# MLP layers: the split, conversion and load of weights are emitted behind a layer-in group instead of in front of it

## The chip, the cores and the metric

The kernel runs on one core of one Trainium2 chip. The metric is the device time of one execution in microseconds (us). TensorE (PE) does the matrix products, VectorE (DVE), ScalarE (ACT) and GpSimd (POOL) the elementwise work, and SyncE (SP) issues the DMAs.

## The reference

```python
def _moe_ref(x, w_in, w_out):                 # x: 1152 tokens x 512
    h = x @ w_in                              # 512 x 2048
    g = np.maximum(0.01 * h, h)
    return (g @ w_out).astype(np.float32)     # 2048 x 512

def _moe2_ref(x, w_in, w_out):
    h = x @ w_in
    g = h * (1.0 / (1.0 + np.exp(-h)))
    return (g @ w_out).astype(np.float32)

def reference(**kwargs):
    attn_out = _attn_ref(**attn_kwargs)       # 2 batches x 8 heads, queries pooled by 2
    x = np.ascontiguousarray(attn_out.transpose(0, 2, 1, 3)).reshape(B * S, H * D)
    x = _moe_ref(x=x, **moe_kwargs)
    return _moe2_ref(x=x, **moe2_kwargs)
```

The four weight matrices arrive as 64-bit floats.

## The kernel before

Attention fills roughly the first 274 us of the program; the two MLP layers fill the rest. The change touches the MLP layers alone.

**Precision and weights.** Every product is made of three matmuls, high by high, high by low and low by high, so each operand exists as a high and a low tile. The weights are cut into 64 *pieces* of 128 x 512. `Weights.load` (L106) fetches one piece as raw 64-bit words into one of 3 buffers. `Weights.convert` turns it into 32-bit floats in one ACT instruction (L127) and four DVE instructions (L131, L135, L139, L145). `Weights.split` makes the high tile on ACT (L163) and the low tile on POOL (L167). The three calls stand together as split, convert, load: the split takes the piece that the call before it converted, the convert takes the next one.

**Units and phases.** A *unit* is (layer, block of the 2048 hidden columns, token group): 2 layers x 4 blocks x 2 groups = 16 units. Group 0 has 512 tokens, group 1 has 640 in two chunks of 320. The loop over `ph` runs 17 *phases*. In phase `ph` the four `layer_in` groups of unit `ph` (here in0 to in3: 12 or 24 matmuls, L923) are interleaved with the output groups of unit `ph - 1` (out0 to out3, or out4: L957 in layer 0, L985 in layer 1) in the order of `phase_order`. The usual one is in0, in1, out0, in2, out1, in3, out2, out3 (, out4). Phase 8 is the first of layer 1; it has in0, in1, out0 to out3, in2, in3. Layer 1 has group 0 in even phases and group 1 in odd ones.

**What follows a group.** In layer 0 ACT alone takes a finished `layer_in` group out of PSUM (L938, L939) and POOL makes the low part `gl` (L944). In layer 1 it takes a chain: a sigmoid on ACT (L941), `a = h * t` on DVE (L942), the copy `gh` on ACT (L943), `gl` on POOL (L944). An output group is added to its accumulator on DVE (L971 in layer 0, L996 in layer 1); for the first block of a layer ACT copies it (L969, L994). At the end of layer 0 each output group is also written as the next layer's input, `xh` on ACT (L973) and `xl` on POOL (L974). The text writes a(ph,i) for the L942 instruction of group in`i` in phase `ph`.

**What sets the order.** In the MLP layers each engine executes its instructions in the order in which this code emits them; there is no planner there. The PSUM pool `ps_p` has 4 buffers, used in rotation by in and out groups alike, so a group on PE starts only when the group four places earlier has been taken out of PSUM. Phases 0 to 2 have a count of weight steps of their own; from phase 3 on there is one split, convert and load for each `layer_in` group until the pieces run out, in phase 14.

Of the kernel before, what the change touches and what calls it, by code (L numbers as in the profile page):

```python
# [18 lines left out]
@with_exitstack  # L19
def pooled_attention_two_mlps(  # L20
    ctx: ExitStack,
    tc: tile.TileContext,
    q: bass.AP,
    k: bass.AP,
    v: bass.AP,
    w1_in: bass.AP,
    w1_out: bass.AP,
    w2_in: bass.AP,
    w2_out: bass.AP,
    out: bass.AP,  # L30
):
    nc = tc.nc
    B, H, S, D = q.shape
    NT, DM = out.shape
    DFF = w1_in.shape[1]
    outer = ctx.enter_context(tc.tile_pool(name="outer", bufs=1))
    KDM = DM // 128
    xh = outer.tile([128, KDM, NT], F32R, name="xh")
    xl = outer.tile([128, KDM, NT], F32R, name="xl")
    weights = Weights(ctx, tc, ((w1_in, w1_out), (w2_in, w2_out)), DM, DFF)  # L40
    with tc.manual_schedule():
        attention(tc, q, k, v, xh, xl, weights)
        mlps(tc, xh, xl, weights, out)
# [20 lines left out]
    weights=(-3.0, -0.3),  # L64
# [827 lines left out]
def mlps(ctx, tc, xh, xl, weights, out):  # L892
# [107 lines left out]
    def phase_order(ph, ins, outs):  # L1000

        if not ins or not outs:
            return ins + outs
        if ph == 2 * NBLK - 1:
            return ins[0:1] + outs[0:2] + ins[1:2] + outs[2:] + ins[2:]
        if ph == 2 * NBLK:
            return ins[0:2] + outs + ins[2:]
        if ph == 4 * NBLK - 1:
            return ins[0:3] + outs[0:1] + ins[3:] + outs[1:]
        order = ins[0:1]  # L1010
        for i in range(max(len(ins) - 1, len(outs))):
            order = order + ins[i + 1:i + 2] + outs[i:i + 1]
        return order
# [4 lines left out]
    for ph in range(len(units) + 1):  # L1018
        ins, outs = [], []
        if ph < len(units):  # L1020
            u = units[ph]
            ins = [(layer_in, u, f) for f in range(FB)]
        if ph > 0:
            w = units[ph - 1]
            if w[0] == 0:
                outs = [(layer_out_t, w, m) for m in range(KDM)]
            else:
                outs = [(layer_out, w, i) for i in range(groups[w[2]][1] * groups[w[2]][2] // 128)]
        order = phase_order(ph, ins, outs)
        for x, u, i in order:  # L1030
            if x is layer_in and ph > 2:
                weights.split()
                weights.convert()
                weights.load()
            x(u, i)
            if x is layer_in and ph == 2:
                weights.split()
                weights.convert()
                weights.load()
            if x is layer_in and ph < 2:  # L1040
                for _ in range((PARAMS["moe0"], PARAMS["moe1"])[ph][i]):
                    weights.convert()
                    weights.load()
                weights.split()
# [29 lines left out]
```

## Time and profile before

| what | value |
|---|---|
| median of 3 runs | 687.91 us (686.66 to 688.94) |
| time of the profiled execution | 688.05 us |
| its span in the trace | 686.3 us |
| mean granted TensorE clock | 0.985 of full speed |
| busy: PE, DVE, POOL, ACT | 657.7, 466.6, 398.9, 321.7 us |

The span is the time between the first and the last recorded instruction; the run's own time is 1.75 us longer. Busy time of an engine is an average over stages that have different limits, so it is read stage by stage below. All times in the rows are us from the start of the span.

### The profile page before, as it was taken

The page shows a single profiled execution, that of the slowest core. Times are in us where ns is not written, and L with a number is a line of the kernel's source. Part 1 is how long each engine was busy: PE and PEld are TensorE (multiplying, and loading weights), DVE is VectorE, ACT ScalarE, POOL GpSimd, SP SyncE. Part 2 cuts the span into 40 slices and gives each one's busy share as a digit, 9 for nine tenths or more (in the row PEclk, how much of TensorE's full clock was granted, in tenths as well). Part 3 has the DMA queues.
Part 4 walks back from the last instruction along what each step waited for, and adds up shares of the span by engine and source line. Part 5 has one row for each costly group of instructions (what it writes and reads, how often), then busy time and mean ns, then how long its engine had stood idle before and what let it go on. Part 6 is the DMA issues. An engine that isn't in the chain of part 4 may idle for free.

```text
span 686.3 us, 10321 instructions
## 1 busy us (share of the span) xinstructions
PE 657.7 (96%) x3741; PEld 533.7 (78%) x3741; DVE 466.6 (68%) x689; ACT 321.7 (47%) x694; POOL 398.9 (58%) x303
## 2 busy tenths in 40 slices
PE   6899999999979988999999999999989999999997
PEld 4566776767756754898988989999878898898986
DVE  6775758577789979497667567367666578877222
ACT  5446667575737555464533334244434543334120
POOL 7476888878868984565454354364634444455220
PEclk9899999999999999999999999999989999999999
DMA  5535151534634123032322223113122322220012
GB/s 147 154 79 140 36 139 37 156 80 125 182 84 120 49 63 105 5 124 93 123 92 78 77 94 91 62 60 95 61 77 78 92 93 69 88 89 1 0 47 92
DMA packets 41898, 59.71 MB, mean 87 GB/s; under 512 B 15324, under 2 KB 24568, under 8 KB 41848
## 3 DMA queue, kind: packets, MB, share of 16 engines
q1 hardware_dynamic: 41848, 59.07, 29.6%
q8 instruction: 29, 0.48, 0.3%
q14 instruction: 21, 0.17, 0.1%
HBM read 49.81 MB, written 2.42 MB: 76 GB/s over the span
## 4 chain that ended last, share of the span: by engine, by line
PE 76%; DVE 13%; issue 4%; ACT 4%; DMA 2%; SPq 1%; ACTq 0%; DVEq 0%
PE ph L923 25%; PE po L957 13%; PE pf L985 12%; PE pss L634 9%; PE pv L666 9%; PE pmx L580 4%; DVE mx L584 3%; PE prep L431 2%; DVE wt L135 2%; DVE wt L139 2%; DVE wt L131 2%; DVE a L942 1%; ACT wt L127 1%; DVE ql L488 1%; DVE wt L145 1%
## 5 line engine op out<-in xcount | busy, mean ns | idle before, releaser
L944 POOL TENSOR_TENSOR gl<-a,gh 128x512 fp32r<-128x512 f32 (+1 forms) x64 | 95.1, 1488 | 163.4 <-ACT gh L943 107.5
L655 POOL TENSOR_TENSOR acc<-acc,e 128x576 f32<-128x576 f32 x105 | 154.7, 1494 | 33.2 <-ACT e L638 27.4
L638 ACT ACTIVATE e<-pss 128x288 f32<-128x288 f32 x288 | 101.8, 411 | 84.9 <-PE pss L634 80.7
L584 DVE TENSOR_REDUCE mx<-pmx 128x1 f32<-128x384 f32 x216 | 110.5, 550 | 33.7 <-PE pmx L580 29.1
L923 PE MATMUL ph<-xh,w0h 128*128 128x320 f32 (+1 forms) x384 | 109.7, 340 | 4.2 <-DVE a L942 3.6
L923 PE MATMUL ph<-xl,w0h 128*128 128x320 f32 (+1 forms) x384 | 109.3, 339 | 0.0
L923 PE MATMUL ph<-xh,w0l 128*128 128x320 f32 (+1 forms) x384 | 109.0, 338 | 0.0
L131 DVE TENSOR_SCALAR wt<-wt 128x512 f32<-128x512 f32 x64 | 51.0, 797 | 81.4 <-ACT wt L127 72.6
L634 PE MATMUL pss<-qh,k 128*128 128x288 f32 x288 | 87.8, 321 | 2.2 <-DVE mx L584 2.0
L666 PE MATMUL pv<-e,vnat 128*64 128x288 f32 x576 | 87.7, 425 | 1.2 <-ACT e L638 1.2
L634 PE MATMUL pss<-ql,ka 128*128 128x288 f32 x288 | 82.2, 301 | 4.3 <-DMA ql<-mn 4.3
L923 PEld LDWEIGHTS ph<-xh,w0h 128*128 128x128 f32 x384 | 68.4, 191 | 12.0 <-DVE a L942 4.7
L923 PEld LDWEIGHTS ph<-xh,w0l 128*128 128x128 f32 x384 | 67.7, 190 | 5.0
L923 PEld LDWEIGHTS ph<-xl,w0h 128*128 128x128 f32 x384 | 67.9, 191 | 4.7
L634 PEld LDWEIGHTS pss<-qh,k 128*128 128x128 f32 x288 | 55.4, 192 | 20.2 <-issue 8.3
L580 PE MATMUL pmx<-k,qh 128*128 128x384 f32 x192 | 66.0, 383 | 4.9 <-DVE mx L584 3.0
L943 ACT ACTIVATE gh<-a 128x512 fp32r<-128x512 f32 (+1 forms) x32 | 22.0, 687 | 95.1 <-DVE a L942 95.1
L145 DVE SCALAR_TENSOR_TENSOR wt<-wraw,wt 128x512 uint32<-128x512 uint32 x64 | 62.6, 978 | 2.0
L135 DVE TENSOR_SCALAR wt<-wt 128x512 uint32<-128x512 uint32 x64 | 62.0, 970 | 2.1
L139 DVE SCALAR_TENSOR_TENSOR wt<-wraw,wt 128x512 uint32<-128x512 uint32 x64 | 58.7, 917 | 2.0
L666 PEld LDWEIGHTS pv<-e,vnat 128*64 128x64 f32 x576 | 35.6, 138 | 31.3 <-issue 14.3
L634 PEld LDWEIGHTS pss<-ql,ka 128*128 128x128 f32 x288 | 55.6, 193 | 5.0 <-DMA ql<-mn 3.0
(76 smaller groups left out, 1126.5 us busy)
## 6 DMA issues: line engine op xcount, KB each, us to landing
wraw<-in_moe_w_in_dram SPq DMA_DIRECT2D x32, 512.0 KB, 3.8
wraw<-in_moe_w_out_dram SPq DMA_DIRECT2D x32, 512.0 KB, 3.3
vnat<-in_v_dram SPq DMA_DIRECT2D x8, 576.0 KB, 4.8
qnat<-in_q_dram SPq DMA_DIRECT2D x16, 256.0 KB, 6.2
knat<-in_k_dram SPq DMA_DIRECT2D x7, 576.0 KB, 4.2
ka<-k SPq DMA_DIRECT2D x16, 160.0 KB, 2.6
out_dram<-acc SPq DMA_DIRECT2D x9, 256.0 KB, 2.0
ka<-k SPq DMA_DIRECT2D x16, 128.0 KB, 2.6
```

The lines of the kernel that those rows point to most:

```text
L135: nc.vector.tensor_scalar(out=t, in0=t, scalar1=4, scalar2=1, op0=ALU.logical_shift_left, op1=ALU.logical_shift_right)
L139: nc.vector.scalar_tensor_tensor(out=t, in0=box["high"], scalar=0x80000000, in1=t, op0=ALU.bitwise_and, op1=ALU.bitwise_or)
L580: nc.tensor.matmul(out=ps[:, 0:KC], lhsT=QH[p, j][:, t * 128:(t + 1) * 128], rhs=K2[p, j][:, ks], start=True, stop=True)
L584: nc.vector.tensor_reduce(out=mx[p][:, n:n + 1], in_=ps[:, 0:KC], op=ALU.max, axis=AX.X)
L634: nc.tensor.matmul(out=ps[:, 0:C], lhsT=lhsT[:, ks], rhs=rhs[:, cs], start=not last, stop=last)
L638: nc.scalar.activation(out=e_t[p, j, t][:, cs], in_=ps[:, 0:C], func=ACTF.Exp, scale=scale)
L655: e.tensor_tensor(out=acc[p, j], in0=e_t[p, j, 0] if t == 1 else acc[p, j], in1=e_t[p, j, t], op=ALU.add)
L666: nc.tensor.matmul(out=vps[p, c][own[j], 0:C], lhsT=vnat[p][:, j, t, :], rhs=e_t[p, j, t][:, c * C:(c + 1) * C], start=(t == 0), stop=(t = ...
L923: nc.tensor.matmul(out=ps[:, c, 0:n], lhsT=wt[:, kk, fs], rhs=m[:, kk, chunk(g, c)], start=(kk == 0 and wt is wh and m is xh), stop=(kk == ...
L944: nc.gpsimd.tensor_tensor(out=gl[:, 0:nch * n], in0=a, in1=gh[:, 0:nch * n], op=ALU.subtract)
L957: nc.tensor.matmul(out=ps[:, c, 0:n], lhsT=wt[:, f, ms], rhs=x[:, c * n:(c + 1) * n], start=(f == 0 and wt is oh and x is gh), stop=(f == ...
L985: nc.tensor.matmul(out=ps[:, 0, :], lhsT=x[:, ts], rhs=wt[:, f, :], start=(f == 0 and x is gh and wt is oh), stop=(f == FB - 1 and x is gl),)
```

## The change

The three weight calls stood ahead of a `layer_in` group for `ph > 2` and behind it for `ph == 2`. Now they stand behind it for every `ph >= 2`. No instruction is added or removed.

```diff
         for x, u, i in order:
-            if x is layer_in and ph > 2:
-                weights.split()
-                weights.convert()
-                weights.load()
             x(u, i)
-            if x is layer_in and ph == 2:
+            if x is layer_in and ph >= 2:
                 weights.split()
                 weights.convert()
                 weights.load()
```

The first place is DVE in phase 12, layer 1, from behind a(12,0) to the accumulation of out1. `a_...` is the product with the sigmoid (L942), `wt_...` the piece in conversion (its four instructions), `pf_...` a finished output group that L996 adds to the accumulator. Before:

```order
L131 TENSOR_SCALAR wt_6097<-wt_6097 128x512
L135 TENSOR_SCALAR wt_6097<-wt_6097 128x512
L139 SCALAR_TENSOR_TENSOR wt_6097<-wraw_5942,wt_6097 128x512
L145 SCALAR_TENSOR_TENSOR wt_6097<-wraw_5942,wt_6097 128x512
L942 TENSOR_TENSOR a_6119<-ph_6105,t_6118 128x512
L996 TENSOR_TENSOR acc1_3469<-pf_6126,acc1_3469 128x512
L131 TENSOR_SCALAR wt_6142<-wt_6142 128x512
L135 TENSOR_SCALAR wt_6142<-wt_6142 128x512
L139 SCALAR_TENSOR_TENSOR wt_6142<-wraw_6001,wt_6142 128x512
L145 SCALAR_TENSOR_TENSOR wt_6142<-wraw_6001,wt_6142 128x512
L942 TENSOR_TENSOR a_6164<-ph_6150,t_6163 128x512
L996 TENSOR_TENSOR acc1_3469<-pf_6171,acc1_3469 128x512
```

The accumulation of an output group stands right behind the product a of the group before it, and in front of the next conversion. The same place with the change:

```order
L942 TENSOR_TENSOR a_6109<-ph_6095,t_6108 128x512
L131 TENSOR_SCALAR wt_6118<-wt_6118 128x512
L135 TENSOR_SCALAR wt_6118<-wt_6118 128x512
L139 SCALAR_TENSOR_TENSOR wt_6118<-wraw_5975,wt_6118 128x512
L145 SCALAR_TENSOR_TENSOR wt_6118<-wraw_5975,wt_6118 128x512
L996 TENSOR_TENSOR acc1_3469<-pf_6126,acc1_3469 128x512
L942 TENSOR_TENSOR a_6154<-ph_6140,t_6153 128x512
L131 TENSOR_SCALAR wt_6163<-wt_6163 128x512
L135 TENSOR_SCALAR wt_6163<-wt_6163 128x512
L139 SCALAR_TENSOR_TENSOR wt_6163<-wraw_6034,wt_6163 128x512
L145 SCALAR_TENSOR_TENSOR wt_6163<-wraw_6034,wt_6163 128x512
L996 TENSOR_TENSOR acc1_3469<-pf_6171,acc1_3469 128x512
```

Now the accumulation stands between the end of a conversion and the next product a.

The second place is DVE in phase 8, where layer 1 begins: from a(8,1) to a(8,2), with the four accumulations of layer 0's last output groups (`po_...`, L971). Before:

```order
L942 TENSOR_TENSOR a_5225<-ph_5211,t_5224 128x512
L971 TENSOR_TENSOR acc1_3469<-po_5232,acc1_3469 128x640
L971 TENSOR_TENSOR acc1_3469<-po_5260,acc1_3469 128x640
L971 TENSOR_TENSOR acc1_3469<-po_5288,acc1_3469 128x640
L971 TENSOR_TENSOR acc1_3469<-po_5316,acc1_3469 128x640
L131 TENSOR_SCALAR wt_5346<-wt_5346 128x512
L135 TENSOR_SCALAR wt_5346<-wt_5346 128x512
L139 SCALAR_TENSOR_TENSOR wt_5346<-wraw_5136,wt_5346 128x512
L145 SCALAR_TENSOR_TENSOR wt_5346<-wraw_5136,wt_5346 128x512
L942 TENSOR_TENSOR a_5368<-ph_5354,t_5367 128x512
```

A conversion stands between the last accumulation and a(8,2). With the change:

```order
L942 TENSOR_TENSOR a_5215<-ph_5201,t_5214 128x512
L131 TENSOR_SCALAR wt_5224<-wt_5224 128x512
L135 TENSOR_SCALAR wt_5224<-wt_5224 128x512
L139 SCALAR_TENSOR_TENSOR wt_5224<-wraw_5124,wt_5224 128x512
L145 SCALAR_TENSOR_TENSOR wt_5224<-wraw_5124,wt_5224 128x512
L971 TENSOR_TENSOR acc1_3469<-po_5232,acc1_3469 128x640
L971 TENSOR_TENSOR acc1_3469<-po_5260,acc1_3469 128x640
L971 TENSOR_TENSOR acc1_3469<-po_5288,acc1_3469 128x640
L971 TENSOR_TENSOR acc1_3469<-po_5316,acc1_3469 128x640
L942 TENSOR_TENSOR a_5358<-ph_5344,t_5357 128x512
```

The conversion has moved ahead of the four accumulations, and a(8,2) follows them directly.

## Rows read from the trace of the kernel before

**Rows 1.** The page: busy us (share of the span) and instructions of PE.

```profile
PE 657.7 (96%) x3741; PEld 533.7 (78%) x3741; DVE 466.6 (68%) x689; ACT 321.7 (47%) x694; POOL 398.9 (58%) x303
```

**Rows 2.** Waits of PE, 425 to 686 us: total us, times, longest us.

```profile
PE ph L923 <- DVE a L942: 3.6, 2, 3.3
```

**Rows 3.** The chain that ended last, from 425 us: start us, us, what.

```profile
506.92 6.51 PE ph L923 x24
...
551.67 2.75 PE pf L985 x12
554.41 3.52 PE ph L923 x24
...
601.25 2.75 PE pf L985 x12
...
635.56 8.16 PE pf L985 x36
```

**Rows 4.** Timeline of phase 12: start us, us, instruction, [idle before <-releaser].

```profile
575.76 0.68 DVE L942 TENSOR_TENSOR a<-ph,t 128x512 f32<-128x512 f32 x1
...
576.48 0.63 ACT L943 ACTIVATE gh<-a 128x512 fp32r<-128x512 f32 x1 [3.42 <-DVE a L942]
...
577.20 1.30 POOL L944 TENSOR_TENSOR gl<-a,gh 128x512 fp32r<-128x512 f32 x1 [3.09 <-ACT gh L943]
...
578.23 0.55 DVE L131 TENSOR_SCALAR wt<-wt 128x512 f32<-128x512 f32 x1 [1.78 <-ACT wt L127]
...
578.46 1.47 POOL L167 TENSOR_TENSOR w1l<-wt,w1h 128x512 fp32r<-128x512 f32 x1
...
581.58 0.68 DVE L942 TENSOR_TENSOR a<-ph,t 128x512 f32<-128x512 f32 x1
...
582.18 0.68 DVE L996 TENSOR_TENSOR acc<-pf,acc 128x512 f32<-128x512 f32 x1
```

**Rows 5.** Timeline of DVE, end of phase 12 to phase 14.

```profile
593.81 1.88 DVE L996 TENSOR_TENSOR acc<-pf,acc 128x512 f32<-128x512 f32 x3
...
599.03 0.82 DVE L942 TENSOR_TENSOR a<-ph,t 128x640 f32<-128x640 f32 x1
...
605.38 0.82 DVE L942 TENSOR_TENSOR a<-ph,t 128x640 f32<-128x640 f32 x1
...
624.38 0.68 DVE L942 TENSOR_TENSOR a<-ph,t 128x512 f32<-128x512 f32 x1
```

**Rows 6.** Timeline of ACT, end of layer 0: in2 of phase 7 leaves PSUM.

```profile
457.07 0.70 ACT L938 ACTIVATE gh<-ph 128x640 fp32r<-128x640 f32 x1 [1.08 <-PE ph L923]
```

**Rows 7.** Timeline of DVE, phases 7 and 8.

```profile
456.10 0.47 DVE L131 TENSOR_SCALAR wt<-wt 128x512 f32<-128x512 f32 x1 [1.85 <-ACT wt L127]
...
458.77 1.95 DVE L145 SCALAR_TENSOR_TENSOR wt<-wraw,wt 128x512 uint32<-128x512 uint32 x1
...
470.36 0.68 DVE L942 TENSOR_TENSOR a<-ph,t 128x512 f32<-128x512 f32 x1
...
480.73 0.82 DVE L971 TENSOR_TENSOR acc<-po,acc 128x640 f32<-128x640 f32 x1 [1.68 <-PE po L957]
...
493.94 0.68 DVE L942 TENSOR_TENSOR a<-ph,t 128x512 f32<-128x512 f32 x1
```

**Rows 8.** Timeline of POOL, phase 8.

```profile
478.86 6.17 POOL L974 TENSOR_TENSOR xl<-acc,xh 128x640 fp32r<-128x640 f32 x4
```

**Rows 9.** DMA issues by line, the page: count, KB each, median us to landing.

```profile
wraw<-in_moe_w_in_dram SPq DMA_DIRECT2D x32, 512.0 KB, 3.8
```

**Rows 10.** Timeline of PE in the attention stage: two waits.

```profile
191.97 0.40 PE L634 MATMUL pss<-qh,k 128*128 128x288 f32 x1 [1.01 <-DVE mx L584]
197.52 0.44 PE L580 MATMUL pmx<-k,qh 128*128 128x384 f32 x1 [2.53 <-DVE mx L584]
```

**Rows 11.** Stretches behind them: us, busy (x count) of each engine, granted clock, DMA share, GB/s.

```profile
192.00:195.00 3.00, 2.97 (x17) 1.76 (x17) 3.00 (x3) 1.12 (x3) 3.00 (x5) 1.00 0.18 53
...
199.00:202.00 3.00, 3.00 (x13) 2.29 (x15) 3.00 (x5) 1.73 (x5) 1.42 (x1) 0.50 0.08 1
```

## Prediction

> **What bounds the kernel now.** The page comes first: PE is busy for 96% of the span [rows 1], so a gain can only come from PE's idle time and a loss only from new idle time. Next the waits of PE from 425 us on: the largest is 3.6 us on L942, one instance of 3.3 us [rows 2]. The chain that ended last shows what that wait did: the group behind it took 6.51 us from 506.92 us, where a group of the same size takes 3.52 us [rows 3]. From 551.67 us on, the chain is nothing but PE to its last matmul, so there PE is the bound.
>
> The timeline of phase 12 shows how near DVE is behind. One turn reads: a(12,0) at 575.76, its `gh` on ACT at 576.48, `gl` on POOL at 577.20, split and convert on ACT, the first DVE step of the conversion at 578.23, the next a at 581.58 [rows 4]. That is a closed loop of 5.82 us through ACT and DVE: ACT converts only behind `gh`, and DVE multiplies only behind the conversion. In group-1 phases the loop is 6.34 us (599.03 to 605.38) [rows 5]. Two phases of eight turns take DVE 48.62 us (575.76 to 624.38) [rows 4, 5]; PE needs 49.58 us for two phases (551.67 to 601.25) [rows 3]. The loop is hidden by 1 us in 50.
>
> In the loop DVE idles for 1.78 us, waiting for the conversion's ACT step, and the accumulations L996 stand in that gap: 582.18, right behind a(12,1) [rows 4], three more at 593.81 in 1.88 us, some 0.6 us each [rows 5]. Before the change they cost nothing.
>
> **The change, part by part.** *The loop itself* keeps its cyclic order (a, `gh`, split, convert, four DVE steps, a), so its 5.82 and 6.34 us stay. The loads stay in one order on SP; each waits for the conversion three turns back, and lands in 3.8 us [rows 9] against two turns of 11.6 us, so DMA costs nothing. If that cover went, a load would be late by what it exceeds 11.6 us.
>
> *The accumulations* are what moves. The first piece of the order shows L996 leaving the place behind a, where it filled the gap, for the place between the conversion's end and the next a. DVE executes its instructions in the order in which they stand, so each adds its 0.6 us to a turn. Behind them in the queue is the next a, and for that wait `gh`, `gl`, the next conversion, and PE through the PSUM buffer. Counts: 4 in phase 11, 5 in 12, 4 in 13. Phases 9 and 10 accumulate nothing on DVE (the first block is copied by ACT), so they add nothing. A pair of phases becomes 48.6 + 9 x 0.6 = 54.0 us against PE's 49.6: DVE becomes the bound, 4.4 us a pair.
>
> Layer 0 has no a on DVE, so its phases 3 to 7 have no such loop: cost 0, covered by PE's groups. If PE ran out of cover there, one split and convert ahead of an ACT copy would be some 1.2 us.
>
> *The start of layer 1.* One conversion fewer stands ahead of a(8,0), but the earlier ones begin later, since they stand behind the copies of phase 7's groups. From ACT's copy of in2 at 457.07 [rows 6]: two copies 1.3, split and convert with DVE's start 1.2, a conversion of 3.4 us (578.23 to 581.58 [rows 4]) or, beside a busy POOL, up to 4.6, once more 1.2 and 3.4. That puts a(8,0) at 467.6 to 468.8, I take 468.2; before it was 470.36 [rows 7]. One turn later a(8,1) is at 474.0, and the conversion that used to stand behind the four accumulations now stands ahead of them (second piece of the order): the first L971 starts at 479.8 and the last ends near 482.9 (0.82 each [rows 7], some 0.1 overlapped), so a(8,2) is at about 484.1. Now POOL is in the way: the four `xl` follow the accumulations and take 6.17 us [rows 8], from some 481.5 to 487.7. `gl` and the split's low part queue behind them (1.26 and 1.47, from 577.20, 578.46 and its length [rows 4]), to 490.4; the conversion ends behind POOL, and a(8,3) follows 1.65 us after POOL in the loop (581.58 less 579.93): 492.1. Before it was 493.94 [rows 7]. So the start gives a lead of 1.8 us. Bounds: no lead (493.94) and a lead of a whole turn, 5.8 us (488.1), which is what the missing conversion is worth if nothing else is late.
>
> *The sum, by DVE's chain.* From a(8,3): 5.82 to phase 9; 4 x 6.34 = 25.4 for it; 4 x 5.82 = 23.3 for phase 10; 25.4 + 2.4 for phase 11; 23.3 + 3.0 for 12; 25.4 + 2.4 for 13; two turns, 11.6, to the first accumulation of phase 14: 148.0 us, or 640.1 us, and 640.8 at its end. Out2 of phase 14 on PE needs that PSUM buffer (four places earlier). Before, it started at 635.56 [rows 3]. From there the pieces have run out and PE sets the pace as before. The end moves by 640.8 - 635.6 = 5.2 us. The sum's base is the profiled execution, 688.05 us, which is 0.14 above the median of the runs: **693.2 us**.
>
> *TensorE's clock.* After a wait of 2.53 us PE ran at a granted clock of 0.50, the level of 1.2 GHz; after one of 1.01 us it stayed at 1.00, 2.4 GHz [rows 10, 11]. The new waits share some 7 us (the 5.2 of the sum and the lead of 1.8) over at least five places in phases 12 to 14, so 1 to 2 us each: between the two rows. I take no fall, being nearer the row without one, and keep one fall for the range: a group at the low level cost 6.51 - 3.52 = 3.0 us [rows 3]. By the Trainium skill (TensorE: Matmul & The Clock Gate, "A second HAM failure mode: psum-queue depth-cycling") frequent short idles of PE between groups, as PSUM banks are cycled through, can make the clock alternate too. That speaks against this change; by the rows short waits have left the clock up, and by the page the time would be the third rival's.
>
> **The rivals.** *Faster: the accumulations stay free.* If DVE still fitted them into its 1.78 us of idle time, the loop would stay at 48.6 us a pair, and the lead of 1.8 us would stand at the start of phase 11, where PE last waited: 686.2 us; with part of the low clock after 506.92 us saved, down to 3.0 us less, 683.2. For it: DVE's total work is unchanged and it idles enough. Against: the order puts a conversion ahead of every accumulation, and that conversion's ACT step is what the idle time waits for. It decides if a turn with an accumulation measures 5.8 and not 6.4.
>
> *No change: the lead pays.* With the whole turn of 5.8 us as lead, the end moves by 5.2 - 4.0 = 1.2 us: 689.3. For it: PE waited for exactly this loop at 506.92. Against: POOL's `xl` block, 6.17 us, now sits between a(8,2) and a(8,3).
>
> *Slower still: the clock falls.* Up to two of the waits in phases 12 to 14 drop the clock. A fall while DVE is the bound is partly hidden, one behind the last wait is not: 3.0 us each at most, 696.2 to 699.2.
>
> **How the numbers follow.** Forecast (691.5 to 695) 0.60, clock 0.20, no change 0.09, faster 0.11. The measurement tells some 0.3%, 2.1 us, from no change, so the forecast and the clock case are slower. A little of the forecast's low end could fall within: faster 0.11, same 0.10, slower 0.79. The range reaches from the edge of the no-change case, 690.3, to one full fall and some, 697.6; it leaves out the faster case and two falls.
>
> **What would show it.** Right: in phases 11 to 13 an L996 directly behind the conversion's last DVE step, a-to-a 6.4 and 6.9 us in turns with one, 5.8 and 6.3 without; DVE's two phases near 54 us; new PE waits in phases 12 to 14, on L996 as well as L942; a(8,3) near 492 and behind POOL's `xl`; the 3.3 us wait in phase 9 shorter. Wrong: L996 running in the gap before the conversion; a(8,3) at 488; a low clock in phases 12 to 14; or a loop shorter than 5.8 us, since one tenth of a us a turn is 2.3 us over its 23 turns.

## The result, and the profile after

The changed kernel takes **693.71 us** (median of 4 runs, 692.26 to 694.30) against 688.20 us of the kernel before beside it (median of 4 runs): a ratio of 1.0079 with a 95% interval from 1.0063 to 1.0094. It is slower by 5.5 us, which is more than the 0.3% that the measurement tells from no change. The forecast of 693.2 us is 0.5 us off. The profiled execution of the changed kernel took 694.30 us, with a span of 692.5 us and a mean granted clock of 0.988.

Two executions differ in their attention stage too, which the change does not touch: the MLP's phase 3 starts on PE at 335.51 us before and at 336.45 us after. So 0.94 us of the two spans' difference is no effect of the change (experiment 1, with the same code as the changed kernel up to that row, has it at 334.18 us). From here on a **stretch** is the time from that first row to the last accumulation (L996), both read from the chain that ended last. Before, these rows are:

```profile
335.51 7.04 PE ph L923 x48
...
682.36 0.69 DVE acc L996
```

That stretch is 346.85 us. The chain of the changed kernel (start us, us, what; answers to [rows 3]):

```profile
336.45 7.04 PE ph L923 x48
...
628.04 1.20 DVE acc L996 x2
632.19 1.41 DVE wt L135
...
641.51 8.46 PE pf L985 x36
...
688.61 0.69 DVE acc L996
```

The stretch is now 352.16 us, 5.31 us more. Before, PE alone made up the chain from 551.67 us on [rows 3]. Now DVE's accumulations and conversions, with ACT's steps between them, make it up to 641.51 us. Behind that row PE sets the pace again.

The waits of PE from 425 us on (line waited for: total us, times, longest us; answer to [rows 2]):

```profile
PE pf L985 <- DVE acc L996: 6.2, 5, 1.6
PE ph L923 <- DVE a L942: 3.7, 3, 2.3
PE ph L923 <- DVE acc L971: 1.0, 1, 1.0
```

The first row is new: an output group on PE waits for an accumulation, because that holds the PSUM buffer it needs. The wait on a, once 3.3 us long in one place [rows 2], is 2.3 us there.

DVE's timeline of the changed kernel, phases 11 to 14 (start us, us, instruction, [idle before <-releaser]; answers to [rows 4, 5]):

```profile
553.86 0.82 DVE L942 TENSOR_TENSOR a<-ph,t 128x640 f32<-128x640 f32 x1
...
560.18 0.68 DVE L996 TENSOR_TENSOR acc<-pf,acc 128x512 f32<-128x512 f32 x1
560.78 0.81 DVE L942 TENSOR_TENSOR a<-ph,t 128x640 f32<-128x640 f32 x1
...
575.22 0.68 DVE L942 TENSOR_TENSOR a<-ph,t 128x512 f32<-128x512 f32 x1
...
581.02 0.68 DVE L942 TENSOR_TENSOR a<-ph,t 128x512 f32<-128x512 f32 x1
583.48 0.55 DVE L131 TENSOR_SCALAR wt<-wt 128x512 f32<-128x512 f32 x1 [1.77 <-ACT wt L127]
...
586.83 0.68 DVE L996 TENSOR_TENSOR acc<-pf,acc 128x512 f32<-128x512 f32 x1
587.43 0.68 DVE L942 TENSOR_TENSOR a<-ph,t 128x512 f32<-128x512 f32 x1
...
629.15 0.68 DVE L942 TENSOR_TENSOR a<-ph,t 128x512 f32<-128x512 f32 x1
...
640.77 0.68 DVE L996 TENSOR_TENSOR acc<-pf,acc 128x512 f32<-128x512 f32 x1
```

A turn without an accumulation still takes 5.80 us (575.22 to 581.02). The next one has an L996 between the conversion's last step and a, and takes 6.41 us (581.02 to 587.43). The idle time behind a is still there, 1.77 us, and now nothing stands in it: the L996 was emitted behind the conversion that DVE is waiting for.

### The profile page after: what moved, and what is told of

Same layout as the page of the kernel before. It is cut to its first block, busy times and chain, and to the rows that moved or that the text cites. A ratio compares the mean times of both kernels' runs of the same rounds, so it can differ in the third digit from the quotient of the medians.

```text
span 692.5 us, 10318 instructions
## 1 busy us (share of the span) xinstructions
PE 657.6 (95%) x3741; PEld 531.1 (77%) x3741; DVE 470.9 (68%) x689; ACT 321.6 (46%) x694; POOL 400.1 (58%) x303
## 4 chain that ended last, share of the span: by engine, by line
PE 60%; DVE 24%; ACT 7%; issue 6%; DMA 2%; SPq 1%; ACTq 0%; DVEq 0%
PE ph L923 16%; PE po L957 12%; PE pss L634 9%; PE pv L666 9%; DVE wt L135 6%; PE pf L985 5%; PE pmx L580 5%; DVE wt L139 3%; DVE wt L131 3%; DVE a L942 3%; DVE mx L584 3%; ACT wt L127 2%; PE prep L431 2%; DVE acc L996 1%; DVE wt L145 1%
## 5 line engine op out<-in xcount | busy, mean ns | idle before, releaser
L131 DVE TENSOR_SCALAR wt<-wt 128x512 f32<-128x512 f32 x64 | 47.3, 738 | 112.3 <-ACT wt L127 103.5
L135 DVE TENSOR_SCALAR wt<-wt 128x512 uint32<-128x512 uint32 x64 | 74.9, 1171 | 2.1
L985 PE MATMUL pf<-w1h,gh 128*128 128x512 f32 x144 | 56.9, 395 | 6.3 <-DVE acc L996 6.2
L145 DVE SCALAR_TENSOR_TENSOR wt<-wraw,wt 128x512 uint32<-128x512 uint32 x64 | 60.1, 940 | 2.0
```

Source lines behind the costliest of these rows:

```text
L131: nc.vector.tensor_scalar(out=tf, in0=tf, scalar1=2.0, scalar2=W_TOP, op0=ALU.max, op1=ALU.min)
L135: nc.vector.tensor_scalar(out=t, in0=t, scalar1=4, scalar2=1, op0=ALU.logical_shift_left, op1=ALU.logical_shift_right)
L985: nc.tensor.matmul(out=ps[:, 0, :], lhsT=x[:, ts], rhs=wt[:, f, :], start=(f == 0 and x is gh and wt is oh), stop=(f == FB - 1 and x is gl),)
```

## The experiments

Four theories stood against each other. **A**: the accumulations now lengthen the loop through ACT and DVE, in which a itself stands. **B**: the weights' pieces come one group later, and that is what costs. **C**: DVE simply has too much to do, wherever its work stands. **D**: the loss is made at the start of layer 1, where POOL's `xl` block sits between a(8,2) and a(8,3). All experiments are edits of the changed kernel. Each stretch is read from one execution; the four kernels with the same code up to phase 10 (changed, 1, 3 and 5) reach a(10,3) 205.19 to 205.26 us behind the stretch's start, so differences of a few tenths of a us can be read.

| kernel | median us (runs) | before beside it | ratio (95% interval) | stretch, us |
|---|---|---|---|---|
| before | | | | 346.85 |
| changed | 693.71 (4) | 688.20 | 1.0079 (1.0063 to 1.0094) | 352.16 |
| 1 no accumulation | 686.15 (10) | 687.59 | 0.9976 (0.9962 to 0.9989) | 344.88 |
| 2 one piece late | 687.79 (10) | 687.59 | 1.0002 (0.9990 to 1.0014) | 346.46 |
| 3 behind, then late | 685.35 (9) | 687.59 | 0.9967 (0.9951 to 0.9982) | 343.87 |
| 4 between a and `gh` | 678.63 (5) | 687.59 | 0.9866 (0.9844 to 0.9889) | 338.12 |
| 5 doubled, changed kernel | 702.92 (4) | 688.03 | 1.0222 (1.0201 to 1.0242) | 361.59 |
| 6 doubled, in the gap | 688.26 (10) | 688.03 | 1.0001 (0.9989 to 1.0013) | 347.18 |
| 7 change from phase 11 | 695.68 (6) | 688.03 | 1.0119 (1.0101 to 1.0138) | 354.52 |
| 8 one piece early | 691.67 (6) | 688.03 | 1.0056 (1.0039 to 1.0073) | 350.15 |

### 1. The change without the 13 accumulations of phases 11 to 13

```diff
-            nc.vector.tensor_tensor(out=a, in0=ps[:, 0, :], in1=a, op=ALU.add)
+            if not (blk == 1 or (blk == 2 and g == 0)):
+                nc.vector.tensor_tensor(out=a, in0=ps[:, 0, :], in1=a, op=ALU.add)
```

> The changed kernel without the 13 accumulations on DVE in phases 11 to 13 (the partial results of those 13 output groups are dropped). Theory A (each accumulation adds 0.6 us to the loop a, gh, convert, a): the loop is back at 48.6 us for two phases, PE no longer waits in phases 12 to 14, and the lead of 1.8 us from the start of layer 1 stays: about 686.4 us. Theory B (the loss comes from weights that are split and converted one group later): nothing changes, about 693.7 us.

The time is 686.15 us, below the kernel before. By the stretch it is 7.28 us below the changed kernel, though every piece comes as late as there. PE's waits from 425 us on in this kernel (its later lines stand one further down):

```profile
...
PE pf L985 <- DVE acc L997: 0.7, 1, 0.7
```

The 6.2 us of waits on an accumulation shrink to the one of 0.7 us that phase 14 keeps. That speaks against B and D, which leave the loss where it is. It does not tell A from C, since leaving work out helps both.

### 2. The weight calls in front of the next layer-in group, behind the output groups

```diff
+            if x is layer_in and pend:
+                weights.split()
+                weights.convert()
+                weights.load()
             x(u, i)
-            if x is layer_in and ph >= 2:
+            pend = x is layer_in and ph >= 3 or x is not layer_in and pend
+            if x is layer_in and 2 <= ph < 3:
                 weights.split()
```

`pend` begins as False. Each piece comes as late against the layer-in groups as in the changed kernel, but the accumulations are emitted ahead of the conversion again, in the gap.

> From phase 3 on the three weight calls stand in front of the next layer_in group, behind the output groups in between: every piece is as late as in the change, but the accumulations stand in the gap behind a again, as before. Theory A: as the kernel before, 688 us within 1 us, a-to-a 5.8 and 6.3 us throughout. Theory B (lateness of the pieces costs): as the change, about 693.7 us.

The time is that of the kernel before (1.0002), and no wait on L996 is left. A later piece alone costs nothing: B falls.

### 3. Behind the group up to phase 10, as experiment 2 from phase 11

```diff
-            pend = x is layer_in and ph >= 3 or x is not layer_in and pend
-            if x is layer_in and 2 <= ph < 3:
+            pend = x is layer_in and ph >= 11 or x is not layer_in and pend
+            if x is layer_in and 2 <= ph < 11:
                 weights.split()
```

(The diff is against experiment 2.)

> The change as it is up to phase 10, where DVE accumulates nothing in layer 1; from phase 11 on the calls stand in front of the next layer_in group. Theory A: the lead of the start of layer 1 is kept and the loop does not grow, so some 1.5 to 2 us under the kernel before, about 686.5 us. Theory B: about 693.7 us.

It is faster than the kernel before, 685.35 us, and by the stretch 2.98 us below it, where 1.5 to 2 were expected. DVE's timeline in phase 12:

```profile
571.55 0.69 DVE L942 TENSOR_TENSOR a<-ph,t 128x512 f32<-128x512 f32 x1
...
577.37 0.68 DVE L942 TENSOR_TENSOR a<-ph,t 128x512 f32<-128x512 f32 x1
577.97 0.68 DVE L996 TENSOR_TENSOR acc<-pf,acc 128x512 f32<-128x512 f32 x1
```

The L996 stands behind a, the turn is 5.82 us, and PE has no wait behind 529.51 us. The start of layer 1 is that of the changed kernel, `xl` block included, and nothing is lost there: D falls.

What nobody expected, some 1 us, is on ACT. In phases 9 and 10 the output groups are copied by ACT (L994) and not added by DVE. ACT's timeline of phase 10 before:

```profile
532.16 0.63 ACT L943 ACTIVATE gh<-a 128x512 fp32r<-128x512 f32 x1 [3.61 <-DVE a L942]
532.70 0.58 ACT L994 ACTIVATE acc<-pf 128x512 f32<-128x512 f32 x1
533.18 0.62 ACT L163 ACTIVATE w1h<-wt 128x512 fp32r<-128x512 f32 x1
```

and in the changed kernel, which has the same calls there as experiment 3:

```profile
536.61 0.63 ACT L943 ACTIVATE gh<-a 128x512 fp32r<-128x512 f32 x1 [3.14 <-DVE a L942]
537.14 0.61 ACT L163 ACTIVATE w1h<-wt 128x512 fp32r<-128x512 f32 x1
537.67 0.65 ACT L127 ACTIVATE wt<-wraw 128x512 f32<-128x512 f32 x1
538.22 0.58 ACT L994 ACTIVATE acc<-pf 128x512 f32<-128x512 f32 x1
```

Before, the copy stands inside the loop, between `gh` and the split; with the calls behind the group it stands behind the conversion's ACT step, in ACT's own idle time. The same edit thus takes ACT's copies out of the loop and puts DVE's accumulations in. Before, such a turn takes 6.09 us (531.45 to 537.54 on DVE); in experiment 3 it takes 5.81 us (528.77 to 534.58). Measured from the start of phase 3, a(8,3) comes 1.79 us earlier than before (491.80 - 335.16 against 493.94 - 335.51), and a(10,3) 2.88 us earlier (540.39 against 543.62, the same way). The difference of 1.1 us is what phases 9 and 10 gave. In experiment 2, which has the copies in the loop but no low clock there, a(8,3) to a(10,3) takes 49.54 us (493.84 to 543.38) against 49.68 before and 48.59 in experiment 3: the copies make up nearly all of it.

### 4. The weight calls between a and `gh` in layer 1

```diff
             nc.vector.tensor_tensor(out=a3, in0=h, in1=t3, op=ALU.mult)
+            weights.split()
+            weights.convert()
+            weights.load()
             nc.scalar.activation(out=gh[:, 0:nch * n], in_=a, func=ACTF.Copy)
...
-            if x is layer_in and ph >= 2:
+            if x is layer_in and 2 <= ph < 2 * NBLK:
```

> In layer 1 the three weight calls stand inside the group, between the product a on DVE and the copy gh on ACT, so that the conversion no longer waits for gh; accumulations stand where the change put them. Theory A (the loss is the length of the loop through ACT and DVE): the loop loses gh and the wait for a, to some 4.9 us a turn and under 47 us for two phases with the accumulations, PE sets the pace through layer 1, and the 3.3 us wait of phase 9 with its low clock goes too: 682 to 685 us. Theory B (pieces late): as the change or little better, 692 to 694 us.

678.63 us, 0.9866 of the kernel before, and better than the 682 to 685 expected. DVE and ACT in phase 12 (later lines stand three further down: `gh` is L946, the accumulation L999):

```profile
574.34 0.69 DVE L999 TENSOR_TENSOR acc<-pf,acc 128x512 f32<-128x512 f32 x1
574.45 0.64 ACT L163 ACTIVATE w1h<-wt 128x512 fp32r<-128x512 f32 x1 [2.13 <-DVE wt L145]
574.94 0.68 DVE L942 TENSOR_TENSOR a<-ph,t 128x512 f32<-128x512 f32 x1
574.99 0.66 ACT L127 ACTIVATE wt<-wraw 128x512 f32<-128x512 f32 x1
575.65 0.63 ACT L946 ACTIVATE gh<-a 128x512 fp32r<-128x512 f32 x1
575.68 1.06 DVE L131 TENSOR_SCALAR wt<-wt 128x512 f32<-128x512 f32 x1
...
579.54 0.68 DVE L999 TENSOR_TENSOR acc<-pf,acc 128x512 f32<-128x512 f32 x1
580.14 0.68 DVE L942 TENSOR_TENSOR a<-ph,t 128x512 f32<-128x512 f32 x1
```

ACT now splits and converts while DVE runs the accumulation and a, no longer behind `gh`, so DVE's first step follows a without the 1.78 us of idle time. A turn with an accumulation takes 5.20 us (4.9 expected). A turn without one takes as long, 5.21 us, as phase 8 of this kernel shows:

```profile
468.33 0.68 DVE L942 TENSOR_TENSOR a<-ph,t 128x512 f32<-128x512 f32 x1
469.66 1.08 DVE L131 TENSOR_SCALAR wt<-wt 128x512 f32<-128x512 f32 x1 [0.65 <-ACT wt L127]
...
473.54 0.69 DVE L942 TENSOR_TENSOR a<-ph,t 128x512 f32<-128x512 f32 x1
```

There DVE idles 0.65 us for ACT's step; in phase 12 the accumulation fills that time. The loop now runs from the conversion's last step over ACT's split and ACT's step to the next conversion, and a is no link of it. So the accumulation is free again in the very place in which it costs 0.6 us a turn in the changed kernel.

Of PE's waits from 425 us on, one is left:

```profile
PE ph L923 <- DVE a L942: 0.6, 1, 0.6
```

DVE does as much as before, in the order of the changed kernel; what is different is the loop. That speaks against C. From 501.99 us on the chain is PE alone to its last matmul, so what is left is PE's own time.

### 5 and 6. The same 13 accumulations done twice, in the loop and in the gap

```diff
             nc.vector.tensor_tensor(out=a, in0=ps[:, 0, :], in1=a, op=ALU.add)
+            if blk == 1 or (blk == 2 and g == 0):
+                nc.vector.tensor_tensor(out=a, in0=ps[:, 0, :], in1=a, op=ALU.add)
```

Experiment 5 has this on the changed kernel, 6 on experiment 2.

> The changed kernel with each of the 13 accumulations of phases 11 to 13 done twice (the partial result is added twice). Theory A (an accumulation behind a conversion lengthens the loop): 13 x 0.6 = 7.8 us on top of the change, about 701.5 us, all of it as waits of PE on L996. Theory C (what counts is DVE's amount of work, not the place): the same addition costs the same here as in the next kernel.

> The kernel whose calls stand in front of the next group (accumulations in the gap behind a), with the same 13 accumulations done twice. Theory A: one more fits into the gap of 1.78 us where one stood; where two or three stand in a row the gap is exceeded by 0.6 and 1.8 us, 3.0 us in all over phases 11 to 13, a part of it covered by the 1 us in 50 that PE has in hand: 688.5 to 690.5 us. Theory C: 7.8 us more than without, about 695.5 us.

The same 13 instructions cost 9.43 us of the stretch in the loop (361.59 - 352.16) and 0.72 us in the gap (347.18 - 346.46). C would have them cost alike, and falls. DVE in experiment 5, phase 12:

```profile
588.94 0.68 DVE L996 TENSOR_TENSOR acc<-pf,acc 128x512 f32<-128x512 f32 x1
589.66 0.69 DVE L998 TENSOR_TENSOR acc<-pf,acc 128x512 f32<-128x512 f32 x1
```

and in experiment 6:

```profile
582.22 0.68 DVE L942 TENSOR_TENSOR a<-ph,t 128x512 f32<-128x512 f32 x1
582.82 0.68 DVE L996 TENSOR_TENSOR acc<-pf,acc 128x512 f32<-128x512 f32 x1
583.54 0.69 DVE L998 TENSOR_TENSOR acc<-pf,acc 128x512 f32<-128x512 f32 x1
584.69 0.55 DVE L131 TENSOR_SCALAR wt<-wt 128x512 f32<-128x512 f32 x1 [0.46 <-ACT wt L127]
...
588.04 0.68 DVE L942 TENSOR_TENSOR a<-ph,t 128x512 f32<-128x512 f32 x1
```

In the gap the second accumulation only eats idle time, of which 0.46 us is left, and the turn stays 5.82 us. Only where two or three output groups stand in a row does a turn grow, by 1.00 us at most (6.82 us, 593.85 to 600.67) and not by the 1.8 expected: L135 takes 0.43 us there, 1.40 us in the other turns. So 688.26 us is a little below the 688.5 to 690.5 expected. In the loop each second accumulation adds 0.72 us rather than 0.6: it reads the tile that the first has just written and starts 0.72 us behind it (588.94 to 589.66), while an a starts 0.60 us behind the L996 ahead of it (586.83 to 587.43 in the changed kernel). 13 x 0.72 is 9.4. That is why 702.92 us stands above the 701.5 expected.

### 7. The change from phase 11 on alone

```diff
+            if x is layer_in and 2 < ph < 11:
+                weights.split()
+                weights.convert()
+                weights.load()
             x(u, i)
-            if x is layer_in and ph >= 2:
+            if x is layer_in and (ph == 2 or ph >= 11):
```

> The calls stand in front of the group up to phase 10, as before, and behind it from phase 11 on. This takes the change's gain at the start of layer 1 away and leaves its loss. Theory A: the product of in0 of phase 11 follows PE at about 548.8 us instead of 550.4, then 93.4 us of lengthened turns to the first accumulation of phase 14: 7.3 us over before, about 695.4 us, slower than the change itself by the lead. Theory D (the loss is made at the start of layer 1, by POOL's xl work in the way): no loss, about 688 us.

The stretch is 7.67 us above the kernel before (7.3 expected). D would have it at the kernel before, some 688 us. The loss comes from phases 11 to 14, and the earlier phases of the change had given part of it back: 2.36 us by these two stretches (354.52 - 352.16).

### 8. The change with one piece more at the end of phase 2

```diff
                 weights.load()
+                if ph == 2 and i == FB - 1:
+                    weights.split()
+                    weights.convert()
+                    weights.load()
```

> The changed kernel with one more split, convert and load at the end of phase 2, so that from phase 3 on every piece comes as early as in the kernel before, and phase 14 has one conversion fewer. Theory A: the loop of phases 11 to 13 is as long as in the change; only the wait of 1.6 us in phase 14 goes with the conversion ahead of it: about 692 us. Theory B (lateness of the pieces costs): back to 688 us.

The stretch is 2.01 us below the changed kernel (1.6 expected): the pieces run out one turn earlier. The waits on an accumulation:

```profile
PE pf L985 <- DVE acc L996: 4.5, 4, 1.6
```

Of the five in the changed kernel the one in phase 14 is gone, 1.64 us. The other four stay, so the loss of phases 11 to 13 does not hang on where the pieces end. Every piece comes as early here as in the kernel before, and the stretch is still 3.30 us above it: against B once more.

## Why the prediction was right

Times of the changed kernel are given less 0.94 us here, so that they stand against the forecast.

- **The loop and the accumulations.** Turns of 5.80 and 6.33 us without an accumulation (5.82 and 6.34 forecast), 6.41 and 6.92 us with one (553.86 to 560.78 for the latter). Phases 12 and 13 take DVE 53.93 us (575.22 to 629.15; 54.0 forecast). Experiments 5 and 6 show that the place is what costs, and not the work.
- **The start of layer 1.** a(8,3) at 492.19 us (492.1 forecast), behind POOL's `xl` block. POOL's timeline there, and DVE's behind the dots:

```profile
482.87 6.19 POOL L974 TENSOR_TENSOR xl<-acc,xh 128x640 fp32r<-128x640 f32 x4 [3.33 <-ACT xh L973]
...
485.89 0.69 DVE L942 TENSOR_TENSOR a<-ph,t 128x512 f32<-128x512 f32 x1 [1.68 <-ACT t L941]
...
490.81 1.67 DVE L139 SCALAR_TENSOR_TENSOR wt<-wraw,wt 128x512 uint32<-128x512 uint32 x1
```

That it comes so near is in part luck: two errors cancel. a(8,2) is at 484.95 us and not at 484.1, because PE waits 1.04 us for the first L971 before it can start in2, and a(8,2) waits for in2 and its sigmoid; the 1.2 us that the forecast puts between the last L971 and a(8,2) come from no row. The turn behind it is 7.24 us and not 8.0: the conversion runs beside POOL's work, slowed (L139 takes 1.67 us, 0.69 in the loop), and a(8,3) starts 1.20 us behind the end of POOL's part of the split and not 1.65.

- **The end.** The first accumulation of phase 14 starts at 639.83 us (640.1 forecast). Out2 behind it starts 5.01 us later than before by the start of phase 3, and its 36 matmuls take 8.46 us where they took 8.16 [rows 3]. Together that is the 5.31 us of the stretch (5.2 forecast).
- **PE's waits.** PE's timeline, the last of the five waits, in phase 14:

```profile
641.51 0.50 PE L985 MATMUL pf<-w1h,gh 128*128 128x512 f32 x1 [1.64 <-DVE acc L996]
```

All waits behind 531 us are on L996, 6.2 us in five places, three in phase 12 and two in phase 14 (some 7 us forecast). None is on L942, where the forecast had some too.
- **The clock.** No fall. Windows of the changed kernel (us, busy of PE, PEld, DVE, ACT, POOL, granted clock, DMA share, GB/s):

```profile
575.00:600.00 25.00, 22.70 (x106) 18.63 (x106) 17.50 (x24) 8.29 (x15) 10.93 (x8) 1.00 0.28 85
...
625.00:650.00 25.00, 22.27 (x98) 17.82 (x97) 15.85 (x22) 7.25 (x13) 10.55 (x8) 1.00 0.00 1
```

The granted clock is 1.00, 2.4 GHz, through both stretches with waits. The section of the Trainium skill that the forecast weighed (TensorE: Matmul & The Clock Gate, "A second HAM failure mode: psum-queue depth-cycling") did not come to bear in the changed kernel: the trace shows five short waits of this kind, 0.68 to 1.64 us, and no change of clock. In experiment 5, whose waits on the accumulations are up to 3.11 us long, the clock did fall.

What was wrong is smaller. The rival "faster" was priced at 686.2 us from the lead of 1.8 us alone; experiment 3, in which the accumulations do stay free, is at 685.35, because ACT's copies leave the loop of phases 9 and 10. The forecast itself did not suffer, since it used the bare loop there. The same rival's "up to 3.0 us less" for the low clock has next to nothing behind it: in experiment 2 the clock stays up at that place and the stretch is 0.39 us shorter than before, so the low clock had been hidden behind DVE's loop. And the wait of 1.04 us on L971 in phase 8 was not foreseen; experiment 3 has it too, 1.01 us, and is faster all the same.

## What to carry to other kernels

When two engines execute in order and hand work to each other, look in the trace for the closed loop between them and for the idle gap in each engine's turn. Independent work emitted so that it falls into the gap is free as far as it fits, as DVE's accumulations were before and ACT's copies were after; emitted between two links of the loop it lengthens every turn, however idle the engine is on average. Which places lie between links is a matter of the loop and not of the instruction: in experiment 4 the place that had cost 0.6 us a turn became free. Best is to shorten the loop itself: with the conversion started ahead of the copy `gh` the kernel takes 0.9866 of the time before.

## What the hardware did that was not expected

TensorE's clock did not follow the length of a wait alone. At the start of phase 9 PE waits for the same a in the kernel before, the changed one and most experiments. Experiment 2 waits as long there as the kernel before (PE's timeline):

```profile
506.82 0.56 PE L923 MATMUL ph<-xh,w0h 128*128 128x320 f32 x2 [3.32 <-DVE a L942]
```

The window behind it, before:

```profile
507.00:513.00 6.00, 6.00 (x23) 6.00 (x24) 3.65 (x5) 2.80 (x5) 2.80 (x2) 0.50 0.26 87
```

and in experiment 2:

```profile
507.00:513.00 6.00, 6.00 (x36) 5.51 (x36) 3.77 (x5) 2.69 (x5) 3.10 (x2) 1.00 0.26 87
```

Before, the clock is at 0.50 (1.2 GHz) after 3.29 us of waiting; in experiment 2 it is at 1.00 (2.4 GHz) after 3.32 us. Shorter waits did both, too. At this same place experiment 3 kept 1.00 after 2.31 us and the changed kernel after 2.30, while experiment 1 had 0.52 from 504 to 507 us, behind 2.31 us. Experiment 5 had 0.50 from 629 to 632 us, behind a wait of 2.02 us, and kept 1.00 after one of 2.36 us at 650.11. What else decides it stays open.

These falls cost next to nothing, as DVE was the bound behind them: experiment 1 reaches a(10,3) 205.19 us behind the start of phase 3, the changed kernel 205.25. In experiment 5, DVE takes 60.43 us for phases 12 and 13 (577.31 to 637.74), which is the changed kernel's 53.93 and 9 x 0.72 within 0.02. For a forecast it means that a wait of 2 to 3.3 us in this kernel gives either clock, and that its price depends on whether another engine is the bound behind it.
